# The low half of a weight unit on GpSimd: one instruction of 1024 columns, or two of 512

## The chip, the cores and the metric

The kernel runs on one core of a Trainium2 chip, as one launch. A core has a tensor engine (PE; its weight loads are listed apart as PEld), a vector engine (DVE), a scalar engine (ACT), GpSimd (POOL) and a sync engine (SP), which here only issues DMAs. The engines run their own instruction streams in order and wait for each other by semaphores. They share one on-chip memory of 128 partitions; matmul results go to a separate accumulation memory that POOL doesn't read here.

The metric is the time of one execution on the device in microseconds, the median over runs. Lower is better.

## The reference, cut to what matters

Attention that keeps only the 32 largest scores of each row, then a mixture of four experts, then a layer that takes the largest of three products. All of it is float32.

```python
scores = scale * np.matmul(q, k.transpose(0, 1, 3, 2))      # 2 batches, 8 heads, 576 x 576
kth = np.partition(scores, -32, axis=-1)[..., -32:-31]
attn = softmax(np.where(scores >= kth, scores, -1e9))
x = np.matmul(attn, v)                                      # -> 1152 tokens x 512
for e in range(4):                                          # w1[e] 512 x 1024, w2[e] 1024 x 512
    out += p[:, e:e + 1] * (np.maximum(x @ w1[e], 0.0) @ w2[e])
h = np.maximum(np.maximum(out @ m1, out @ m2), out @ m3)    # each 512 x 768
return h @ m_out                                            # 768 x 512
```

## The kernel before, in words

**High and low parts.** PE multiplies float32 operands in a format with fewer bits. To keep the accuracy, an operand is split in two: `hi`, a rounded copy that ACT writes, and `lo = raw - hi`, a subtraction. A product then takes three matmuls (`product`, L588 to L590): with the low part of one operand, with both high parts, and with the low part of the other. Tokens, hidden values and weights are all split so.

**Weight units.** The weights come as units of 128 x 1024 float32 (512 KB), 176 of them over the program. `w_units` lists them in the order in which the products use them. A unit goes through four steps:

1. SP loads it into one of three buffers (`raw`, L176). The load waits until the buffer's last readers are done, which are ACT's copy and the subtraction of the unit three places earlier.
2. ACT writes `whi` (L225, 1024 columns, one instruction).
3. POOL writes `wlo = raw - whi` (L229, 1024 columns, one instruction). From the phase with index `LATE` on (about two thirds of the way through the program), every second unit goes to DVE instead: POOL writes 136 units and DVE 40.
4. PE uses `whi` and `wlo` from one of five buffers each.

`weight` calls `w_split_to` for the unit wanted and four more (`W_AHEAD`), so that steps 1 to 3 stand in the program some units ahead of the products.

**The order of the work.** Nothing is reordered by a scheduler: each engine runs its instructions as the Python code emits them. `attention` runs through 36 pairs of heads and tiles in time slots. For each head of a pair, PE makes the scores, DVE finds the 32 largest by four MAX8 (L370) and three MATCH_REPLACE8 (L372) of 576 columns, ACT takes the exponential, and a mask sets what is too small to zero. For the first pairs the mask is POOL's (L393, L394); for the other 57 heads it is one DVE instruction (L390, `p = (s >= kth) * p`, which reads `s` and `p`, both in on-chip memory, and adds up the row). PE then transposes `p` (L408) and multiplies with the values.

Between the slots `products` emits the matmuls of the experts and of the last layer. How many go between two slots is decided by a clock kept in Python, which adds up what DVE and PE are thought to take (`dve`, `pe`, `clock`). It knows column counts only, not waits. From slot 306 on the weights of the last layer, which come as 64-bit floats, are turned into 32-bit ones in 48 pieces (`to_float32`), by three DVE instructions of each (L199, L202, L205) and an integer addition on POOL (L208), and stored to a buffer in DRAM from which they are loaded as units later.

POOL's other work stands in the same stream as `wlo`: low parts of the tokens (`xl`, L474), of the keys and queries (`kT` L261, `ql` L293), of some hidden values (L661, L795) and small memsets.

**What the change and the prediction touch.** The subtraction in `w_split_to` (L229), its readers on PE (L588 for the second kind of unit, L590 for the first), the load that waits for it (L176), and the DVE instructions with two inputs from on-chip memory that run beside it (L390, L199, L202, L205, L229 on DVE).

Of the kernel before, what the change touches and what calls it, by code (L numbers as in the profile page):

```python
# [10 lines left out]
F32 = mybir.dt.float32  # L11
# [4 lines left out]
ALU = mybir.AluOpType  # L16
# [34 lines left out]
def kernel(  # L51
# [14 lines left out]
    nc = tc.nc  # L66
# [103 lines left out]
    def w_load_to(n):  # L170
        while w_pos["load"] < min(n, len(order)):
            key, src = order[w_pos["load"]]
            if key[1] in "cd" and narrowed[0] < WIDE * (narrow_at[key[2:]] + 1):
                return
            raw = wp.tile([P, 1024], F32, tag="raw", bufs=3, name="raw")
            nc.sync.dma_start(out=raw, in_=src)  # L176
            w_raw[key] = raw
            w_pos["load"] += 1
# [37 lines left out]
    def w_split_to(n):  # L216
        while w_pos["split"] < min(n, len(order)):
            w_load_to(w_pos["split"] + 1)
            if w_pos["load"] == w_pos["split"]:
                return  # L220
            key, src = order[w_pos["split"]]
            raw = w_raw.pop(key)
            hi = wp.tile([P, 1024], F32R, tag="hi", name="whi")
            lo = wp.tile([P, 1024], F32R, tag="lo", name="wlo")
            nc.scalar.activation(out=hi, in_=raw, func=AF.Copy)  # L225

            late = w_pos["split"] - w_index[PHASES[LATE][1], "c" if PHASES[LATE][0] == 2 else "a", 0, 0]
            on = nc.vector if late >= 0 and late % 2 else nc.gpsimd
            on.tensor_tensor(out=lo, in0=raw, in1=hi.bitcast(F32), op=ALU.subtract)  # L229
            f = 512 if key[1] in "bd" else 256  # L230
            w_hl[key] = (hi.rearrange("p (a f) -> p a f", f=f), lo.rearrange("p (a f) -> p a f", f=f))
            w_pos["split"] += 1
            w_load_to(w_pos["split"] + 2)

    def weight(key, oldest=None):

        w_split_to(w_index[oldest or key] + W_AHEAD)
        return w_hl[key]
# [585 lines left out]
    for s, done in attention():  # L824
        if s == 20:
            load_gates()
        if s == W_FIRST - 12:
            w_load_to(3)
        if W_FIRST <= s < W_FIRST + 16 and not (s - W_FIRST) % 4:
            w_split_to((s - W_FIRST) // 4 + 1)  # L830
        if s == W_FROM - 6:
            for i in range(AHEAD_S):
                wide_load(i)
        if s >= W_FROM + W_STEP * conv and conv < WIDE * len(wide):
            converting.append(to_float32(conv))
            conv += 1
        for x in list(converting):
            if next(x, 0) == 0:
                converting.remove(x)
        split_waiting()  # L840
        assert not any((x.c, x.hp) in done for x in waiting)
        x_ready.update(done)
        clock["goal"] += (clock["dve"] - before) * SHARE[min(phase[0], len(SHARE) - 1)]
        before = clock["dve"]
        while clock["pe"] < clock["goal"]:
            if not advance():
                clock["pe"] = clock["goal"]
# [67 lines left out]
```

## Time and profile before

| what | value |
| --- | --- |
| median of 3 runs | 808.96 us (807.49 to 810.57) |
| the profiled execution | 808.2 us |
| its span, first to last instruction | 806.4 us |
| mean granted TensorE clock | 0.943 of full speed |
| PE busy | 746.3 us, 93% |
| DVE busy | 683.8 us, 85% |
| POOL busy | 527.2 us, 65%, of which `wlo` 336.5 us in 136 instructions |
| ACT busy | 492.7 us, 61% |
| DMA | 126.24 MB, mean 157 GB/s |

The span is the stretch that the trace covers; the profiled execution took 1.8 us more than it. A matmul's busy time runs past the start of the next one, since they are pipelined, so PE's share is higher than the share of the time that its matmuls need. The shares are means over stages with different limits: attention ends at about 490 us, and the products run on to the end.

### The profile page before, as it was taken

The numbers are of one execution on the slowest core, as the hardware profiler recorded it, in microseconds if no ns is written. First come the engines' busy times: TensorE is split into PE (matmuls) and PEld (weight loads), VectorE is DVE, ScalarE is ACT, GpSimd is POOL, SyncE is SP. The second block draws the span as 40 slices with busy tenths as digits, with TensorE's granted clock in tenths as the row PEclk, the third lists the DMA queues.
The fourth block names the chain that finished last, engine by engine and source line by source line (L and its number), as shares of the span: only waits on it lengthen the run. The fifth ranks groups of instructions, "written<-read, shape, count | busy, mean of one in ns | idle before, by whom it ended". The sixth has DMA issues, their size and how long they took to land.

```text
span 806.4 us, 13973 instructions
## 1 busy us (share of the span) xinstructions
PE 746.3 (93%) x4942; PEld 663.2 (82%) x4942; DVE 683.8 (85%) x1242; ACT 492.7 (61%) x1027; POOL 527.2 (65%) x316
## 2 busy tenths in 40 slices
PE   3776799999999989999999999989999898999998
PEld 2454699888898879888888987879988697989996
DVE  6999989999999999999999996999999683445441
ACT  5666768677776775766777665665565444545541
POOL 2787968779888876668777685566565473555330
PEclk8556599999999999999999999999999899999999
DMA  3430245636545445253534364877777455656531
GB/s 98 117 106 13 68 131 147 190 117 173 174 137 171 135 146 151 88 169 112 161 126 146 112 188 152 270 249 250 245 251 243 157 178 167 232 165 208 178 102 40
DMA packets 50214, 126.24 MB, mean 157 GB/s; under 512 B 7904, under 2 KB 18144, under 8 KB 50144
## 3 DMA queue, kind: packets, MB, share of 16 engines
q1 hardware_dynamic: 41936, 116.69, 46.8%
q10 hardware_dynamic: 8208, 8.65, 3.1%
q8 instruction: 39, 0.64, 0.3%
q14 instruction: 31, 0.25, 0.1%
HBM read 116.67 MB, written 8.65 MB: 155 GB/s over the span
## 4 chain that ended last, share of the span: by engine, by line
DVE 41%; PE 35%; DMA 8%; issue 6%; POOL 4%; ACT 4%; SPq 2%; ACTq 0%; DVEq 0%; POOLq 0%
DVE m L370 14%; DVE work L372 13%; PE ps L588 9%; PE ps L590 9%; PE ps L589 9%; DVE p L390 6%; DMA narrow<-narrow 3%; POOL wlo L229 2%; DMA raw<-in_w_dram 2%; DVE h L668 2%; ACT whi L225 2%; SPq L246 2%; DMA kraw<-in_k_dram 1%; PE pso L590 1%; PE pso L588 1%
## 5 line engine op out<-in xcount | busy, mean ns | idle before, releaser
L229 POOL TENSOR_TENSOR wlo<-raw,whi 128x1024 fp32r<-128x1024 f32 x136 | 336.5, 2487 | 162.6 <-ACT whi L225 155.8
L225 ACT ACTIVATE whi<-raw 128x1024 fp32r<-128x1024 f32 x176 | 182.9, 1058 | 73.7 <-DMA raw<-narrow 23.8
L588 PE MATMUL ps<-xl,whi 128*128 128x256 f32 (+1 forms) x512 | 155.3, 303 | 1.7 <-DVE h L668 0.8
L370 DVE MAX8 m<-work 128x8 f32<-128x576 f32 x216 | 154.6, 742 | 0.1
L589 PE MATMUL ps<-xh,whi 128*128 128x256 f32 (+1 forms) x512 | 152.6, 298 | 0.0
L590 PE MATMUL ps<-xh,wlo 128*128 128x256 f32 (+1 forms) x512 | 152.6, 298 | 0.0
L229 DVE TENSOR_TENSOR wlo<-raw,whi 128x1024 fp32r<-128x1024 f32 x40 | 61.6, 1541 | 66.4 <-ACT whi L225 64.9
L372 DVE MATCH_REPLACE8 work<-m,work 128x576 f32<-128x576 f32 x144 | 106.4, 740 | 0.0
L588 PEld LDWEIGHTS ps<-xl,whi 128*128 128x128 f32 x512 | 99.0, 193 | 3.7 <-DVE h L668 1.3
L589 PEld LDWEIGHTS ps<-xh,whi 128*128 128x128 f32 x512 | 98.8, 193 | 0.9
L590 PEld LDWEIGHTS ps<-xh,wlo 128*128 128x128 f32 x512 | 98.7, 193 | 0.0
L590 PE MATMUL ps<-x2h,wlo 128*128 128x256 f32 (+1 forms) x288 | 85.4, 296 | 0.8 <-DVE wlo L229 0.8
L588 PE MATMUL ps<-x2l,whi 128*128 128x256 f32 (+1 forms) x288 | 85.3, 296 | 0.0
L589 PE MATMUL ps<-x2h,whi 128*128 128x256 f32 (+1 forms) x288 | 85.2, 296 | 0.0
L390 DVE SCALAR_TENSOR_TENSOR p<-s,m,p 128x576 f32<-128x576 f32 x57 | 81.0, 1422 | 0.0
L588 PE MATMUL ps<-wlo,h 128*128 128x512 f32 x192 | 77.7, 405 | 0.0
L590 PE MATMUL ps<-whi,h 128*128 128x512 f32 x192 | 75.3, 392 | 0.0
L589 PE MATMUL ps<-whi,h 128*128 128x512 f32 x192 | 75.3, 392 | 0.0
L408 PE MATMUL psp<-ident,p 128*128 128x128 f32 x288 | 50.8, 306 | 26.3 <-POOL p L394 15.4
L208 POOL TENSOR_TENSOR narrow<-narrow,raw 128x256 int32<-128x256 int32 x48 | 41.2, 858 | 44.7 <-DVE narrow L205 14.6
L349 PE MATMUL pss<-kT,ql 128*128 128x288 f32 x160 | 55.1, 358 | 13.9 <-DVE ql L293 7.6
L408 PEld LDWEIGHTS psp<-ident,p 128*128 128x128 f32 x288 | 38.3, 156 | 32.9 <-POOL p L394 18.9
(104 smaller groups left out, 1706.0 us busy)
## 6 DMA issues: line engine op xcount, KB each, us to landing
raw<-in_w_dram SPq DMA_DIRECT2D x128, 512.0 KB, 3.9
raw<-narrow SPq DMA_DIRECT2D x48, 512.0 KB, 3.8
raw<-in_m_dram SPq DMA_DIRECT2D x36, 256.0 KB, 4.4
narrow<-narrow ACTq DMA_DIRECT2D x48, 128.0 KB, 3.7
kraw<-in_k_dram SPq DMA_DIRECT2D x14, 288.0 KB, 4.5
raw<-in_mo_dram SPq DMA_DIRECT2D x12, 256.0 KB, 4.2
vt<-in_v_dram SPq DMA_DIRECT2D x8, 288.0 KB, 4.2
out_dram<-ob ACTq DMA_DIRECT2D x9, 256.0 KB, 2.0
```

The source lines that it names most:

```text
L208: nc.gpsimd.tensor_tensor(out=out.bitcast(I32), in0=out.bitcast(I32), in1=last, op=ALU.add)
L225: nc.scalar.activation(out=hi, in_=raw, func=AF.Copy)
L229: on.tensor_tensor(out=lo, in0=raw, in1=hi.bitcast(F32), op=ALU.subtract)
L246: nc.sync.dma_start(out=out[half * D:(half + 1) * D], in_=src)
L349: nc.tensor.matmul(ps[:, 0:SH], lhsT=l, rhs=r, start=i == 0, stop=i == len(mm) - 1)
L370: nc.vector.max(m[:, 8 * r:8 * r + 8], src)
L372: nc.vector.match_replace(out=self.w[j], in_to_replace=m[:, 8 * r:8 * r + 8], in_values=src, imm_value=NEG)
L390: nc.vector.scalar_tensor_tensor(out=p, in0=s, scalar=kth, in1=p, op0=ALU.is_ge, op1=ALU.mult, accum_out=total)
L408: nc.tensor.transpose(ps[:, r * P:(r + 1) * P], self.p[:, part, part * TAIL + r * P:part * TAIL + (r + 1) * P], ident)
L588: nc.tensor.matmul(ps, lhsT=lh, rhs=rl, start=first, stop=False)
L589: nc.tensor.matmul(ps, lhsT=lh, rhs=rh, start=False, stop=False)
L590: nc.tensor.matmul(ps, lhsT=ll, rhs=rh, start=False, stop=last)
```

## The change

The subtraction on POOL is made by two instructions, the first for columns 0 to 511 and the second for columns 512 to 1023 of the same unit. Where the subtraction is DVE's, it stays one instruction. Buffers, DMAs and all other work are the same.

```diff
             late = w_pos["split"] - w_index[PHASES[LATE][1], "c" if PHASES[LATE][0] == 2 else "a", 0, 0]
             on = nc.vector if late >= 0 and late % 2 else nc.gpsimd
-            on.tensor_tensor(out=lo, in0=raw, in1=hi.bitcast(F32), op=ALU.subtract)
+
+            for x in (slice(0, 512), slice(512, 1024)) if on is nc.gpsimd else (slice(0, 1024),):
+                on.tensor_tensor(out=lo[:, x], in0=raw[:, x], in1=hi[:, x].bitcast(F32), op=ALU.subtract)
             f = 512 if key[1] in "bd" else 256
```

Two lines are added, so a line below it has a number higher by two after the change. No engine's order changes; the waits do at three places.

POOL's stream, early in the first product phase, before (`DMAHW`, `Activation`, `PE` name the semaphores of the DMA queues, ACT and PE):

```order
62 L229 TENSOR_TENSOR wlo<-raw,whi 128x1024 [waits DMAHW3_49,Activation_49]
63 L229 TENSOR_TENSOR wlo<-raw,whi 128x1024 [waits DMAHW4_49,PE_49,Activation_49]
64 L229 TENSOR_TENSOR wlo<-raw,whi 128x1024 [waits DMAHW5_49,PE_49,Activation_49]
65 L229 TENSOR_TENSOR wlo<-raw,whi 128x1024 [waits DMAHW6_49,PE_49,Activation_49]
66 L293 TENSOR_TENSOR ql<-qraw,qh 128x2x256 [waits DMAHW2_49,DMAHW1_49,Activation_49]
```

The same place after the change:

```order
66 L231 TENSOR_TENSOR wlo<-raw,whi 128x512 [waits DMAHW3_49,Activation_49]
67 L231 TENSOR_TENSOR wlo<-raw,whi 128x512
68 L231 TENSOR_TENSOR wlo<-raw,whi 128x512 [waits DMAHW4_49,PE_49,Activation_49]
69 L231 TENSOR_TENSOR wlo<-raw,whi 128x512
70 L231 TENSOR_TENSOR wlo<-raw,whi 128x512 [waits DMAHW5_49,PE_49,Activation_49]
71 L231 TENSOR_TENSOR wlo<-raw,whi 128x512
72 L231 TENSOR_TENSOR wlo<-raw,whi 128x512 [waits DMAHW6_49,PE_49,Activation_49]
73 L231 TENSOR_TENSOR wlo<-raw,whi 128x512
74 L295 TENSOR_TENSOR ql<-qraw,qh 128x2x256 [waits DMAHW2_49,DMAHW1_49,Activation_49]
```

The first of the two carries the waits of the old one; the second has none.

PE's stream at the third unit, whose first four products use columns in the order of the unit, before:

```order
203 L590 MATMUL ps_1071<-xh,wlo 128x256 [waits Pool_49]
204 L588 MATMUL ps_1071<-xl,whi 128x256
205 L589 MATMUL ps_1071<-xh,whi 128x256
206 L590 MATMUL ps_1071<-xh,wlo 128x256
207 L588 MATMUL ps_1071<-xl,whi 128x256
208 L589 MATMUL ps_1071<-xh,whi 128x256
209 L590 MATMUL ps_1071<-xh,wlo 128x256
```

After the change:

```order
203 L592 MATMUL ps_1075<-xh,wlo 128x256 [waits Pool_49]
204 L590 MATMUL ps_1075<-xl,whi 128x256
205 L591 MATMUL ps_1075<-xh,whi 128x256
206 L592 MATMUL ps_1075<-xh,wlo 128x256
207 L590 MATMUL ps_1075<-xl,whi 128x256
208 L591 MATMUL ps_1075<-xh,whi 128x256
209 L592 MATMUL ps_1075<-xh,wlo 128x256 [waits Pool_49]
```

The first matmul with `wlo` now waits for the first half alone, and the one that reads columns from 512 on waits for the second. On SP the loads of later units wait for ACT's semaphore too, which before was covered by the wait for POOL's.

## Rows read from the trace of the kernel before

**Rows 1.** Busy time by stretch: us, PE, PEld, DVE, ACT, POOL, PEclk, DMA share, GB/s

```profile
85.00:190.00 105.00, 97.74 (x707) 87.09 (x707) 101.38 (x206) 74.39 (x167) 83.26 (x48) 0.92 0.45 134
190.00:490.00 300.00, 290.47 (x2210) 256.90 (x2209) 292.16 (x592) 206.88 (x452) 227.20 (x120) 0.99 0.50 149
490.00:640.00 150.00, 144.18 (x715) 128.37 (x715) 138.86 (x196) 86.24 (x168) 89.14 (x67) 0.99 0.71 228
640.00:740.00 100.00, 97.47 (x721) 92.54 (x721) 51.31 (x54) 48.61 (x65) 50.01 (x27) 0.98 0.57 190
```

**Rows 2.** The chain that ended last, by line, 190 to 490 us

```profile
by line: DVE m L370 28.9%; DVE work L372 26.4%; DVE p L390 17.2%; issue 5.2%; DVE h L668 4.4%; DVE acc L697 2.7%; PE ps L588 1.7%; DMA raw<-in_w_dram 1.7%; ACT whi L225 1.7%; PE ps L590 1.7%; PE ps L589 1.7%; DVE xt L461 1.2%; ACT pt L411 0
```

**Rows 3.** DVE's L390 as a group, 190 to 490 us: busy us, mean ns, idle before

```profile
L390 DVE SCALAR_TENSOR_TENSOR p<-s,m,p 128x576 f32<-128x576 f32 x43 | 60.2, 1401 | 0.0
```

**Rows 4.** DVE's L390 in order of time: start us, duration us

```profile
92.69 2.65 DVE L390 SCALAR_TENSOR_TENSOR p<-s,m,p 128x576 f32<-128x576 f32 x1
...
201.23 0.81 DVE L390 SCALAR_TENSOR_TENSOR p<-s,m,p 128x576 f32<-128x576 f32 x1
...
215.29 2.79 DVE L390 SCALAR_TENSOR_TENSOR p<-s,m,p 128x576 f32<-128x576 f32 x1
...
223.04 2.32 DVE L390 SCALAR_TENSOR_TENSOR p<-s,m,p 128x576 f32<-128x576 f32 x1
...
483.27 2.26 DVE L390 SCALAR_TENSOR_TENSOR p<-s,m,p 128x576 f32<-128x576 f32 x1
```

**Rows 5.** POOL in order of time: start us, duration us, in brackets idle time before

```profile
92.39 2.35 POOL L229 TENSOR_TENSOR wlo<-raw,whi 128x1024 fp32r<-128x1024 f32 x1
94.69 1.79 POOL L293 TENSOR_TENSOR ql<-qraw,qh 128x512 fp32r<-128x512 f32 x1
...
202.62 4.76 POOL L229 TENSOR_TENSOR wlo<-raw,whi 128x1024 fp32r<-128x1024 f32 x2 [2.06 <-ACT whi L225]
...
215.07 2.40 POOL L229 TENSOR_TENSOR wlo<-raw,whi 128x1024 fp32r<-128x1024 f32 x1
217.43 0.97 POOL L474 TENSOR_TENSOR xl<-xt,xh 128x128 fp32r<-128x128 f32 x1
...
222.33 5.29 POOL L229 TENSOR_TENSOR wlo<-raw,whi 128x1024 fp32r<-128x1024 f32 x2
227.58 0.46 POOL L474 TENSOR_TENSOR xl<-xt,xh 128x128 fp32r<-128x128 f32 x1
```

**Rows 6.** Durations by line, ns: min/median/max, first and last start us

```profile
L229 POOL TENSOR_TENSOR wlo<-raw,whi x136: 2351/2410/3290, 86.2 to 780.0; 128x1024 fp32r<-128x1024 f32 x136
...
L202 DVE TENSOR_SCALAR narrow<-raw x48: 277/730/2495, 491.9 to 659.4; 128x256 uint32<-128x256 uint32 x48
L205 DVE SCALAR_TENSOR_TENSOR narrow<-raw,narrow x48: 409/425/2628, 492.2 to 660.6; 128x256 uint32<-128x256 uint32 x48
...
L661 POOL TENSOR_TENSOR h<-raw,h x12: 1272/1294/1952, 127.3 to 493.6; 128x512 fp32r<-128x512 f32 x12
```

**Rows 7.** One matmul group of PE, 190 to 490 us: busy us, mean ns

```profile
L588 PE MATMUL ps<-xl,whi 128*128 128x256 f32 x284 | 82.4, 290 | 1.7 <-DVE h L668 0.8 <-ACT raw L659 0.5 <-ACT r L438 0.2
```

**Rows 8.** One matmul of that shape in the chain that ended last

```profile
102.89 0.12 PE ps L588
```

**Rows 9.** POOL's `wlo` as a group, 190 to 490 us: busy, mean, idle before

```profile
L229 POOL TENSOR_TENSOR wlo<-raw,whi 128x1024 fp32r<-128x1024 f32 x72 | 178.2, 2495 | 57.5 <-ACT whi L225 56.3 <-DMA raw<-in_w_dram 0.9
```

**Rows 10.** The chain that ended last, by line, 85 to 190 us

```profile
by line: POOL wlo L229 12.9%; issue 12.7%; PE ps L588 10.6%; PE ps L589 10.6%; PE ps L590 10.5%; DMA raw<-in_w_dram 10.2%; SPq L246 5.8%; PE psp L408 3.8%; DVE m L370 3.7%; PE pss L349 3.5%; PE psv L451 2.9%; DVE work L372 2.8%; POOL kT L26
```

**Rows 11.** PE's waits for `wlo` of L229, whole run: us, times

```profile
  PEld ps L590: 1.2, 2
  PE ps L590: 0.8, 2
```

**Rows 12.** PE's longest waits, 490 us to the end: us, times, longest us

```profile
PE ps L588 <- DVE acc L697: 5.4, 2, 3.2
...
PE ps L590 <- DVE wlo L229: 0.8, 2, 0.4
```

**Rows 13.** PE's longest wait, 190 to 490 us: us, times, longest us

```profile
PE psp L408 <- DVE p L390: 3.5, 3, 2.5
```

## The prediction

> **What bounds the kernel now.** I read the busy time by stretch first [rows 1]. From 190 to 490 us, the longest stage, DVE is busy for 292.16 of 300 us and PE for 290.47; POOL has 73 us to spare. From 490 us on PE is the fullest engine (144.18 of 150 us, then 97.47 of 100). The chain that ended last says the same of the long stage: DVE's top-32 and mask lines L370, L372 and L390 alone are 72.5% of it, and L390 is 17.2% [rows 2]. The reader is to see there that `wlo` on POOL is not in the chain of this stage, so that making `wlo` slower or faster would not matter by itself.
>
> What matters is L390. Its 43 instructions take 1401 ns on the mean [rows 3], yet one of the same size takes 0.81 us when POOL is idle: it starts at 201.23 us [rows 4], and POOL's next instruction begins at 202.62 after 2.06 us of idle time [rows 5]. So 43 x (1.401 - 0.81) = 25.4 us of DVE's time in this stage is spent waiting inside L390. For what, the instructions side by side show. At 215.29 us L390 starts 0.22 us after a `wlo` on POOL and takes 2.79 us; that `wlo` is not lengthened (2.40 us) and ends at 217.47, and L390 ends 0.61 us later [rows 4, 5]. At 223.04 us it starts 0.71 us after a `wlo` and takes 2.32 us, again to some 0.6 us behind that `wlo`'s end [rows 4, 5]. DVE's instruction with two inputs from on-chip memory does not run beside POOL's: it waits until the POOL instruction under way is over. The turn then is DVE's, even with POOL's next instruction ready: the two `wlo` from 222.33 take 5.29 us together, 0.49 us more than 2 x 2.40, and the `xl` at 217.43 takes 0.97 us where the one at 227.58 takes 0.46 [rows 5]. POOL pays about 0.5 us for each such turn.
>
> **The change, part by part.** *What a half costs.* POOL's subtraction of 1024 columns has a median of 2.41 us, one of 512 columns (L661) of 1.29 us [rows 6]. Two halves are 2.58 us. Consecutive POOL instructions overlap a little: the one at 92.39 ends at 94.74 and the next has begun at 94.69, so 0.05 us comes off [rows 5]. A unit costs POOL 2 x 1.29 - 0.05 - 2.41 = 0.12 us, taken as 0.13, and 136 of them 17.7 us.
>
> *What DVE saves from 190 to 490 us.* A DVE instruction that comes during the first half now waits for 1.29 us at most instead of 2.41, so it is let through 1.12 us earlier. One that comes during the second half waits as before. In the old trace those of the first kind are the L390 that took over 0.81 + 1.12 = 1.93 us. I count ten of the 43, the first at 215.29 and the last at 483.27 [rows 4]: 10 x 1.12 = 11.2 us.
>
> *How much of it reaches the end.* PE is nearly as busy as DVE in this stage, and its matmuls are spread between the slots by a clock that doesn't know of DVE's waits, so they don't move. If DVE keeps its share, all 11.2 us go. If PE can't go above 99% busy, the stage takes 290.47 / 0.99 = 293.4 us and 6.6 us go. PE has in truth more room than that: a matmul of 256 columns is listed with 290 ns [rows 7], but in the chain one follows another after 0.12 us [rows 8], so its busy time covers small holes. I take the middle, **8.9 us**, and keep 3.5 and 11.2 as the ends: 3.5 us is what PE itself waits for L390 here [rows 13], the least that an earlier L390 gives back.
>
> *POOL in this stage.* 72 units x 0.13 = 9.4 us more, and 0.5 us for each turn that DVE now takes between two halves, ten of them. POOL sits idle for 57.5 us before its `wlo` here, nearly all of it waiting for ACT [rows 9]; that covers it. Without that cover, each unit would come 0.13 us later.
>
> *From 85 to 190 us.* Here POOL's `wlo` is the largest item of the chain, 12.9% of 105 us, some 5.6 units [rows 10]. These cost 5.6 x 0.13 = 0.7 us, and up to three turns of DVE in mid-unit 0.5 us each. Against that three L390 took over 1.93 us (the first, at 92.69 [rows 4], 2.65 us), worth 3.4 us of DVE's time, most of it not in the chain. I put this at 0, between 3.4 us gained and 2.2 us lost.
>
> *From 490 us on.* The conversion of the last weights has more such DVE instructions: L202 takes 277 ns at least and up to 2495, L205 409 and up to 2628 [rows 6]. DVE will be freer, but PE is the bound. What PE waits for DVE is 5.4 us in two waits for L697 and 0.8 us for DVE's own `wlo` [rows 12]. I take 1 us gained, between 0 and 6.2.
>
> *The new waits.* PE's first use of `wlo` now waits for half a unit, the later ones for the rest. PE lost 0.8 us to `wlo` of either engine in the whole run, and PEld 1.2 us [rows 11], since units are made some way ahead: at most that much to gain, nothing to lose. The extra wait on SP for ACT's copy has long been met when POOL's second half is done: 0.
>
> *The sum.* 8.9 + 0 + 1 = 9.9 us. The profiled execution took 808.2 us and would take 798.3. It is 0.76 us below the median of the runs, 808.96, to which I refer the forecast: **799.1 us**.
>
> **The rivals.** *(a) No gap between the halves.* All turns that the trace shows are given to DVE in front of a POOL instruction that has waits of its own. The second half has none. If it follows so closely that DVE isn't let in, DVE waits for both halves and each wait grows by 0.13 us: 35 of the 57 L390 begin inside a `wlo` (the first at 92.69, the last at 483.27 [rows 4]), 4.6 us, and 0.7 us on POOL's chain before 190 us: 808.96 + 5.3 = **814.3 us**, slower. What decides is whether DVE can start at all between two halves. Against it stands that the second of two `wlo` whose waits had been met let DVE in, and that such pairs overlap by the same 0.05 us [rows 5]. The Trainium skill (GPSIMD Engine Reference, section Instruction dispatch) speaks for it: each of GpSimd's cores begins the next instruction as soon as it has done its own share of the one before, and completion holds back only who waits for it. By that rule the sum would be that of this rival; the turn at 222.33 us [rows 5] is against it so far.
>
> *(b) PE takes over.* With PE at 290.47 of 300 us [rows 1], DVE's gain may turn into waiting for PE, at the next point where a score or a product is needed. Then only PE's own 3.5 us of waiting for L390 [rows 13] come off: **805.5 us**, no change within the bound below. For it: the two engines' near equal load. Against it: the holes inside PE's busy time [rows 7, 8].
>
> *(c) All of it counts.* PE's stream closes up, the stage gives its 11.2 us, the last stages the 5.4 us that PE waits for L697 [rows 12], and the stage before 190 us 1 us: 808.96 - 17.6 = **791.4 us**.
>
> **How the numbers follow.** Forecast 64%, (b) 16%, (a) 11%, (c) 9%. Half a per cent, 4.0 us, is about what a measurement of this kernel can tell from no change, so 804.9 and 813.0 are the limits. The forecast and (c) are faster: 73%. (b) is no change: 16%. (a) is slower: 11%. The range reaches from 790 us, just beyond (c), to 807 us, just beyond (b); it leaves out (a) and the tails of the others, and holds the ends of the costly terms: 3.5 us gained in the long stage alone gives 805.5, all bounds on the good side together (11.2 + 3.4 + 6.2) 788.2, which I leave out.
>
> **What would show it.** In the new profile POOL's halves should have a median near 1.29 us and a sum some 18 us above the 336.5 us of now. L390 should fall from 1.40 us on the mean in the long stage to about 1.14 (11.2 us less over 43), and its longest from 2.79 us and more to about 1.8; a longest still near 2.8 means rival (a). Attention should end some 9 us earlier; if L390 is shorter and attention ends as late as now, with more waiting of DVE for PE or ACT, it is (b). POOL's idle time before `wlo` should shrink but stay well above zero; if it is gone, or PE's waits for `wlo` go up by several us, I have misjudged POOL's cover and the forecast is wrong.

## The result, and the profile after

| what | before | after |
| --- | --- | --- |
| median of 4 runs | 808.23 us (806.68 to 810.57) | 796.33 us (795.39 to 797.97) |
| ratio of the times, 95% interval | | 0.9857 [0.9831, 0.9883] |
| the profiled execution, its span | 808.2, 806.4 us | 795.39, 793.6 us |
| POOL's `wlo` | 336.5 us in 136 | 374.9 us in 272 |

The change is faster by 1.4%, 11.9 us. The forecast was 799.1 us in a range from 790 to 807. A line below the edit has a number higher by two: DVE's mask is L392, the subtraction L231.

Busy time by stretch after the change (columns as in [rows 1]):

```profile
85.00:190.00 105.00, 96.72 (x721) 86.08 (x722) 101.41 (x208) 75.22 (x170) 88.45 (x73) 0.96 0.46 137
190.00:490.00 300.00, 294.89 (x2248) 262.06 (x2248) 291.70 (x602) 214.15 (x464) 245.19 (x198) 1.00 0.51 150
490.00:640.00 150.00, 144.96 (x755) 130.38 (x754) 135.72 (x197) 86.11 (x166) 96.56 (x85) 0.99 0.76 242
640.00:740.00 100.00, 97.47 (x704) 91.04 (x703) 43.88 (x49) 45.83 (x60) 54.52 (x40) 1.00 0.54 182
```

In the long stage PE gets through 2248 matmuls in 300 us instead of 2210, and DVE through 602 instructions instead of 592. POOL is 18 us busier there.

The mask and the subtraction as groups, 190 to 490 us (busy us, mean ns, idle time before):

```profile
L392 DVE SCALAR_TENSOR_TENSOR p<-s,m,p 128x576 f32<-128x576 f32 x43 | 53.5, 1243 | 0.0
...
L231 POOL TENSOR_TENSOR wlo<-raw,whi 128x512 fp32r<-128x512 f32 x146 | 198.5, 1390 | 43.7 <-ACT whi L225 43.0 <-POOL narrow L208 0.5
```

The 43 masks take 53.5 us where they took 60.2 [rows 3]. POOL's idle time before `wlo` went from 57.5 [rows 9] to 43.7 us, so its cover was drawn on and is not used up.

Durations by line over the whole run (min, median, max in ns):

```profile
L231 POOL TENSOR_TENSOR wlo<-raw,whi x272: 1266/1299/2312, 86.0 to 768.6; 128x512 fp32r<-128x512 f32 x136
L202 DVE TENSOR_SCALAR narrow<-raw x48: 275/726/1390, 480.6 to 645.9; 128x256 uint32<-128x256 uint32 x48
...
L392 DVE SCALAR_TENSOR_TENSOR p<-s,m,p x57: 797/1287/1936, 92.5 to 474.2; 128x576 f32<-128x576 f32 x57
```

The longest mask is 1.94 us, against 2.79 us and more [rows 4]; the longest L202 fell from 2.50 [rows 6] to 1.39 us. Nothing on DVE waits for a whole unit any more. L202 reads one tensor (`high`), though the section on the kernel before and the prediction take it for an instruction with two inputs. It waits all the same: before, 35 of its 48 instructions took over 0.4 us, where the least is 0.28, and each of these ends 0.15 or 0.16 us behind the end of a POOL instruction.

How the turn is taken, in order of time (start us, duration us), POOL first and then DVE's masks:

```profile
214.53 3.04 POOL L231 TENSOR_TENSOR wlo<-raw,whi 128x512 fp32r<-128x512 f32 x2
217.53 0.46 POOL L476 TENSOR_TENSOR xl<-xt,xh 128x128 fp32r<-128x128 f32 x1
...
214.54 1.89 DVE L392 SCALAR_TENSOR_TENSOR p<-s,m,p 128x576 f32<-128x576 f32 x1
...
221.38 1.26 DVE L392 SCALAR_TENSOR_TENSOR p<-s,m,p 128x576 f32<-128x576 f32 x1
```

This is nearly the place of the mask at 215.29 in [rows 4]. The mask comes as POOL starts a unit; the first half, at its median of 1.30 us, ends at 215.83, and the mask ends at 216.43, 0.60 us behind it. Before, a mask ended 0.61 us behind the whole unit. The two halves together take 3.04 us, 0.49 us more than 2 x 1.30 - 0.05: POOL's second half waited for the mask. The `xl` behind them takes its plain 0.46 us, where it took 0.97 [rows 5]. The turn has moved from the unit's end to its middle. This is no single case: of the masks from 190 to 490 us, the 27 before and the 28 after that took over 0.9 us all end 0.61 or 0.62 us behind the end of a POOL instruction.

The chain that ended last, by line, 190 to 480 us:

```profile
by line: DVE m L372 24.7%; DVE work L374 22.8%; DVE p L392 13.0%; PE ps L590 5.7%; PE ps L592 5.7%; PE ps L591 5.7%; DVE h L670 4.0%; issue 3.8%; PE psv L453 2.6%; DVE acc L699 2.1%; PE pss L351 1.8%; DMA raw<-in_w_dram 1.8%; PE psp L410 1.
```

DVE still leads, with the mask at 13.0% instead of 17.2% (the window before is 190 to 490 us, since attention ended later there), but PE's three products have gone from 5.1% [rows 2] to 17.1%: the two engines now share the stage's end.

Where the time came from: I take three marks, the starts of the 16th and of the 57th (last) mask and the end of the span. Before they are 201.23 and 483.27 [rows 4] and 806.4 us; after, the two masks are

```profile
200.25 0.81 DVE L392 SCALAR_TENSOR_TENSOR p<-s,m,p 128x576 f32<-128x576 f32 x1
...
474.20 1.31 DVE L392 SCALAR_TENSOR_TENSOR p<-s,m,p 128x576 f32<-128x576 f32 x1
```

So the way to the 16th mask gave 1.0 us, the stretch between the marks 282.0 - 273.9 = 8.1 us, and the rest 323.1 - 319.4 = 3.7 us: 12.8 us, the difference of the spans. The change run once more (below) has the marks at 203.6 and 476.5 of 795.8 us, which is -2.4, 9.1 and 3.8 us. The first part is thus within what differs from run to run; the second and third repeat.

### The profile page after: what moved, and what is told of

Read it like the earlier page. It is cut to its first block, busy times and chain, and to the rows that moved or that the text cites. A ratio compares the mean times of both kernels' runs of the same rounds, so it can differ in the third digit from the quotient of the medians.

```text
span 793.6 us, 14150 instructions
## 1 busy us (share of the span) xinstructions
PE 737.1 (93%) x4942; PEld 656.4 (83%) x4942; DVE 666.1 (84%) x1242; ACT 492.8 (62%) x1027; POOL 557.5 (70%) x452
## 4 chain that ended last, share of the span: by engine, by line
DVE 44%; PE 33%; DMA 8%; issue 6%; POOL 4%; ACT 4%; SPq 1%; ACTq 0%; DVEq 0%; POOLq 0%
DVE m L372 16%; DVE work L374 14%; PE ps L590 8%; PE ps L592 8%; PE ps L591 8%; DVE p L392 6%; POOL wlo L231 3%; DMA raw<-in_w_dram 2%; ACT whi L225 2%; DMA raw<-narrow 2%; DVE h L670 2%; PE pso L592 1%; PE pso L590 1%; DMA raw<-in_m_dram 1%; PE pso L591 1%
## 5 line engine op out<-in xcount | busy, mean ns | idle before, releaser
L231 POOL TENSOR_TENSOR wlo<-raw,whi 128x512 fp32r<-128x512 f32 x272 | 374.9, 1406 | 140.2 <-ACT whi L225 129.0
L231 DVE TENSOR_TENSOR wlo<-raw,whi 128x1024 fp32r<-128x1024 f32 x40 | 57.4, 1435 | 76.5 <-ACT whi L225 71.9
L392 DVE SCALAR_TENSOR_TENSOR p<-s,m,p 128x576 f32<-128x576 f32 x57 | 73.4, 1288 | 0.0
L351 PE MATMUL pss<-kT,ql 128*128 128x288 f32 x160 | 55.0, 358 | 13.5 <-DVE ql L295 7.5
L410 PEld LDWEIGHTS psp<-ident,p 128*128 128x128 f32 x288 | 37.4, 153 | 30.3 <-POOL p L396 18.8
```

The lines of the kernel that those rows point to most:

```text
L231: on.tensor_tensor(out=lo[:, x], in0=raw[:, x], in1=hi[:, x].bitcast(F32), op=ALU.subtract)
L351: nc.tensor.matmul(ps[:, 0:SH], lhsT=l, rhs=r, start=i == 0, stop=i == len(mm) - 1)
L392: nc.vector.scalar_tensor_tensor(out=p, in0=s, scalar=kth, in1=p, op0=ALU.is_ge, op1=ALU.mult, accum_out=total)
L410: nc.tensor.transpose(ps[:, r * P:(r + 1) * P], self.p[:, part, part * TAIL + r * P:part * TAIL + (r + 1) * P], ident)
```

## The experiments

My theory (T): a mask waits for the POOL instruction under way, halves let DVE in earlier, and DVE's time in attention is the gain. The rivals: the gain comes from what an extra instruction does beside that (an earlier release of half a unit to PE, waits of a finer grain); or from the conversion after attention; or DVE's gain is capped by PE. All edits are to the changed kernel, on its loop `for x in ...` unless shown otherwise; each ratio is to the kernel before, run on the same chip.

**Quarters.**

```diff
-            for x in (slice(0, 512), slice(512, 1024)) if on is nc.gpsimd else (slice(0, 1024),):
+            for x in [slice(i, i + 256) for i in range(0, 1024, 256)] if on is nc.gpsimd else (slice(0, 1024),):
```

> Four instructions of 256 columns per unit on GpSimd. Theory T (DVE gets its turn at the end of each GpSimd instruction, so shorter ones make it wait less): the mask on DVE (0.81 us undisturbed, mean 1.40 us before and 1.24 us with halves in the stretch from 190 to 490 us) falls to 1.0 to 1.1 us; GpSimd pays about 0.4 us more per unit than with one instruction (55 us in all), which fills its idle time but for the stretch before 190 us; time 790 to 797 us. Rival P (PE or the loads gain because a unit's first columns are released earlier; DVE's waits have nothing to do with it): a further gain of about half the first, 788 to 792 us, with the mask unchanged at 1.24 us. Rival C (fewer slow-clock stretches of TensorE by chance): 796 to 808 us, unrelated to the mask.

Measured: 800.37 us, 0.9902 [0.9872, 0.9932], a miss: both the time and the mean mask, 1194 ns, lie above what T expects. (The time lies where chance with the clock would put it, too, but the six runs' clocks, 0.951 to 0.972, are those of the change, 0.950 to 0.973.) The masks did get shorter than with halves, the kernel's time didn't:

```profile
L231 POOL TENSOR_TENSOR wlo<-raw,whi 128x256 fp32r<-128x256 f32 x289 | 220.0, 798 | 27.8 <-ACT whi L225 24.2 <-DMA raw<-in_w_dram 2.8 <-PE ps L590 0.2
L392 DVE SCALAR_TENSOR_TENSOR p<-s,m,p 128x576 f32<-128x576 f32 x43 | 51.4, 1194 | 0.0
```

These are the groups from 190 to 490 us. POOL has 27.8 us of idle time left where the halves have 43.7: a quarter has a median of 742 ns, so a unit costs 4 x 0.742 - 3 x 0.05 - 2.41 = 0.41 us more than in one piece. And something new happened, in order of time:

```profile
439.46 7.74 POOL L231 TENSOR_TENSOR wlo<-raw,whi 128x256 fp32r<-128x256 f32 x11
447.14 0.48 POOL L476 TENSOR_TENSOR xl<-xt,xh 128x128 fp32r<-128x128 f32 x1
447.56 2.81 POOL L231 TENSOR_TENSOR wlo<-raw,whi 128x256 fp32r<-128x256 f32 x4
457.39 0.74 POOL L231 TENSOR_TENSOR wlo<-raw,whi 128x256 fp32r<-128x256 f32 x1 [7.02 <-ACT whi L225]
446.22 4.77 DVE L392 SCALAR_TENSOR_TENSOR p<-s,m,p 128x576 f32<-128x576 f32 x1
```

The mask that comes at 446.22 is kept out past the ends of several POOL instructions and ends at 450.99, 0.62 us behind the last of them (447.56 + 2.81 = 450.37), after which POOL is idle. It got no turn in between. (This execution took 806.69 us, the longest of the six.) Rival (a) of the prediction, refuted for the halves, does occur here, for single masks.

**A cut at column 64**, `(slice(0, 64), slice(64, 1024))`: an extra instruction and the same waits, but nearly the old length for a mask to wait for. No read of PE lies in the first 64 columns (it takes `wlo` by 128 or 512 columns), so this cut releases nothing to PE early.

> Two instructions per unit as in the change, but of 64 and 960 columns: the added instruction, its cost and its waits without a cut in the middle. Theory T: DVE's mask stays at 1.35 to 1.40 us, because 960 columns hold DVE almost as long as 1024; GpSimd's pair costs about 0.13 us more than one instruction; time 806 to 811 us. Rival that two instructions or the finer waits help by themselves: 795 to 799 us as with the change.

Measured: 810.23 us, 1.0005 [0.9983, 1.0026]. The masks, 190 to 490 us:

```profile
L392 DVE SCALAR_TENSOR_TENSOR p<-s,m,p 128x576 f32<-128x576 f32 x43 | 62.5, 1453 | 0.0
```

They are no shorter than the 1401 ns of [rows 3] (and a little longer than expected), and no time is gained. The extra instruction is worth nothing by itself; the length of the piece is what counts. The early release is tried below, with the second half first.

**Halves in attention alone, halves after it alone**, by `and late < 0` and `and late >= 0` behind `on is nc.gpsimd` (the second kind leaves attention's units whole).

> Halves only for the 96 units before DVE takes a share of the units, that is as long as attention runs; one instruction for the 40 later ones. Theory T with the split of the gain that the traces show (attention's end 11 us earlier, the rest 1 to 2 us): 797 to 800 us, mask 1.2 to 1.27 us. If the gain came mainly from the later stages: 804 to 808 us.

> Halves only for the 40 units on GpSimd after attention; one instruction for the 96 earlier ones. Theory T: mask 1.40 us as before, 806 to 809 us, since PE is the fullest engine there and DVE's shorter waits are covered. If the late stages carry the gain: 797 to 802 us.

Measured: 798.37 us, 0.9861 [0.9836, 0.9886], and 806.4 us, 0.9975 [0.9951, 0.9998]. The masks of the first, then of the second:

```profile
L392 DVE SCALAR_TENSOR_TENSOR p<-s,m,p 128x576 f32<-128x576 f32 x43 | 53.3, 1239 | 0.0
```

```profile
L392 DVE SCALAR_TENSOR_TENSOR p<-s,m,p 128x576 f32<-128x576 f32 x43 | 60.2, 1400 | 0.0
```

The gain lies in attention. The halves after it, where DVE's conversion runs beside them, are worth about a quarter of a per cent, with an interval that nearly reaches nothing.

**POOL without reads.** How much would be gained if DVE never had to wait for `wlo`? POOL writes zeros into `wlo` instead of subtracting, in one piece of 1024 columns. Of the edit, which is to the kernel before, the loop around it and the old subtraction behind `else` are not shown.

```diff
+                if on is nc.gpsimd:
+                    on.memset(lo[:, x].bitcast(F32), 0.0)
+                else:
```

> GpSimd fills the low parts of its 136 units with zeros by one memset of 1024 columns, which reads nothing, instead of subtracting; the low parts of these weights are left out of the products. It shows how much more DVE's waiting is worth than halves give back. Theory T: a GpSimd instruction that only writes does not hold DVE up, so the mask takes 0.81 us but for the few behind other GpSimd instructions, mean below 0.9 us from 190 to 490 us (18 us less of DVE's time than with halves). If DVE stays the bound of that stretch, attention ends 25 us earlier than before and the time is 778 to 786 us; if PE takes over, as its 294.9 busy us of 300 with halves suggest, 786 to 794 us. If the mask stays at 1.2 us or more, what DVE waits for is not the reading, and T needs mending.

Measured: 777.54 us, 0.9619 [0.9587, 0.9651], below both ranges that were expected. The mask and POOL's memset in order of time, then the mask's group and the stretch 190 to 490 us:

```profile
233.57 1.85 POOL L232 MEMSET wlo<- 128x1024 f32 x2
...
234.17 0.81 DVE L395 SCALAR_TENSOR_TENSOR p<-s,m,p 128x576 f32<-128x576 f32 x1
```

```profile
L395 DVE SCALAR_TENSOR_TENSOR p<-s,m,p 128x576 f32<-128x576 f32 x42 | 36.2, 862 | 0.0
```

```profile
190.00:490.00 300.00, 299.54 (x2269) 267.52 (x2268) 280.26 (x609) 217.35 (x469) 117.20 (x126) 1.00 0.51 156
```

The mask runs beside a memset in its plain 0.81 us. The chain from 190 us to the end of attention here is PE's:

```profile
by line: PE ps L595 23.1%; PE ps L593 22.9%; PE ps L594 22.9%; PE pss L354 8.7%; PE psv L456 8.2%; PE psp L413 6.5%; PE psv L459 3.0%; PE psr L441 2.0%; PE psp L418 0.8%; POOL h L666 0.7%; ACT whi L225 0.3%; ACT s L362 0.3%; ACT h L665 0.2%
```

From the 16th to the 57th mask (191.7 and 462.7 us) it takes 271.0 us, 11.0 less than before, with PE at 299.54 of 300 us. That is what PE leaves to be gained in this stretch; the halves' 8.1 and 9.1 us are most of it. The rest of this kernel's gain lies ahead of the 16th mask, which comes 9.5 us earlier than before, and behind attention. It does two things at once there, less work for POOL and no waiting of DVE, so it doesn't say which of them gives it.

**DVE's own units in halves too**: the condition `if on is nc.gpsimd else ...` is dropped.

> As the change, and DVE's own 40 subtractions in two halves as well, so that GpSimd gets a turn in their middle. Theory T: GpSimd waits less behind DVE, but in the stages after attention, where PE is the fullest engine; DVE pays some 0.1 us more per unit, 4 us in all, off the path: 795 to 798 us, the same as the change within the error. If turns matter there too, 792 to 794 us.

Measured: 801.7 us, 0.9919 [0.9887, 0.995], a miss. (The interval just overlaps that of the change in its second measurement below, so the loss against the change is at the edge of the noise.) DVE's subtraction as a group from 490 us on, first of this kernel, then of the changed one:

```profile
L231 DVE TENSOR_TENSOR wlo<-raw,whi 128x512 fp32r<-128x512 f32 x78 | 67.5, 906 | 67.7 <-ACT whi L225 64.4 <-issue 3.3
```

```profile
L231 DVE TENSOR_TENSOR wlo<-raw,whi 128x1024 fp32r<-128x1024 f32 x39 | 55.6, 1426 | 74.1 <-ACT whi L225 69.5 <-POOL wlo L231 3.1 <-issue 1.5
```

Two halves on DVE are 1.81 us on the mean against 1.43 for the whole. By their medians, 0.692 us for a half and 1.226 for a whole, the second instruction itself costs 0.16 us; the other 0.22 us is time beyond the medians, which I take for waits, since each half can meet a POOL instruction. Attention ends as with the change (the 57th mask at 475.9 us), so the loss lies behind it, in an execution of 804.89 us, the longest of its six.

**Thirds**, pieces of 352, 336 and 336 columns.

> Three instructions of 352, 336 and 336 columns. Theory T with two opposite terms: DVE's mask falls between that of halves (1.24 us from 190 to 490 us) and that of quarters (1.10 us without one outlier), GpSimd pays another 0.13 to 0.2 us per unit; quarters measured 800 us and halves 796 us, so 795 to 799 us. Outside that, the two terms do not explain the quarters.

Measured: 795.97 us, 0.9848 [0.9817, 0.9879]: the masks' mean goes down to 1218 ns, the time is that of the halves. One mask misses its turns here as well; in order of time:

```profile
373.75 5.36 POOL L231 TENSOR_TENSOR wlo<-raw,whi 128x352 fp32r<-128x352 f32 x6
379.06 0.47 POOL L476 TENSOR_TENSOR xl<-xt,xh 128x128 fp32r<-128x128 f32 x1
379.48 2.67 POOL L231 TENSOR_TENSOR wlo<-raw,whi 128x352 fp32r<-128x352 f32 x3
377.32 5.45 DVE L392 SCALAR_TENSOR_TENSOR p<-s,m,p 128x576 f32<-128x576 f32 x1
```

It ends at 382.77, again 0.62 us behind the end of POOL's run at 382.15.

**The second half first**, `(slice(512, 1024), slice(0, 512))`, so that PE's first matmul with `wlo` waits for both halves as before.

> The same two halves, the second half of the columns first, so that PE's first use of a unit waits for both and its early release is gone. Theory T: nothing is lost, 795 to 798 us, mask 1.2 to 1.27 us from 190 to 490 us, because PE waited 0.8 us for these units in the whole run. Rival P, early release: 802 to 808 us.

Measured: 797.98 us, 0.9877 [0.9847, 0.9906], with a mean mask of 1197 ns. PE's waits for `wlo` are 1.2 us in 4 and PEld's 2.1 us in 4, against 0.8 and 1.2 us in 2 each: less than 1.5 us in all. The early release of the first half is not the source of the gain.

**POOL's other long subtractions in halves too**: `ql` (L295) head by head, the hidden values' low part (L663) in two, beside the change. The second edit is not shown.

```diff
-        sub(out=l, in0=t[:, heads, 0:n], in1=h.bitcast(F32), op=ALU.subtract)
+        for j in range(h.shape[1]):
+            sub(out=l[:, j], in0=t[:, heads, 0:n][:, j], in1=h[:, j].bitcast(F32), op=ALU.subtract)
```

> The change, and GpSimd's low parts of the queries and of its hidden values in two instructions each as well (768 and 512 columns become 2 x 384 and 2 x 256). Theory T: the waits of DVE's mask behind these, 2.7 us in the change's trace from 190 to 490 us, fall by about 1.3 us, and those of the conversion behind the hidden values (5.7 us) by half, the latter off the path; GpSimd pays 31 x 0.13 = 4 us. 794 to 797 us, so not to be told from the change; mask 1.20 to 1.25 us. A gain of 4 us or more would mean that turns behind long instructions matter more than their sum says.

Measured: 796.8 us, 0.9867 [0.984, 0.9895]; the masks of 190 to 490 us fall further, below what was expected:

```profile
L393 DVE SCALAR_TENSOR_TENSOR p<-s,m,p 128x576 f32<-128x576 f32 x43 | 50.2, 1167 | 0.0
```

That is 3.3 us less of DVE than with the change, and none of it shows in the time of the whole. Between the marks some of it does: from the 16th to the 57th mask this kernel takes 271.8 us, the two traces of the change 273.9 and 272.9, and the kernel without POOL's reads 271.0. Here PE leads the chain from 190 to 480 us, with 46.5% for its three products:

```profile
by line: PE ps L593 15.5%; PE ps L591 15.5%; PE ps L592 15.5%; DVE m L373 11.8%; DVE work L375 11.2%; DVE p L393 5.9%; PE psv L454 5.2%; PE pss L352 4.9%; PE psp L411 4.3%; PE psv L457 1.9%; DVE h L671 1.7%; issue 1.6%; PE psr L439 1.4%; DV
```

What lies behind the 57th mask is 323.2 us, longer than the change's 319.4, in an execution of 800.5 us, the longest of its six.

**The change, the quarters and the thirds once more**, beside the last one; the latter two as one execution each. Was the long mask of the quarters chance, and what is the scatter?

> The change unaltered, in the same job as the others, for comparison with the kernels of earlier jobs: ratio to before 0.983 to 0.988, 794 to 798 us; mask 1.20 to 1.28 us from 190 to 490 us, none of its 57 instructions above 2.0 us.

> The quarters again, for one look. In their first trace one mask at 446 us took 4.77 us: GpSimd's next six instructions ran in front of it. If a turn is missed by the program's order, the same mask (the 52nd of 57) is above 4 us again; if it hangs on timing by nanoseconds, another one or none is. The rest of the masks as before, median 0.9 to 1.1 us, time 798 to 807 us.

> The thirds again, for one look. In their first trace one mask at 377 us took 5.45 us. As for the quarters: the same mask again if the program's order makes it, another or none if it hangs on timing. Time 794 to 800 us.

Measured: the change 796.96 us, 0.9872 [0.985, 0.9893], with a mask mean of 1223 ns and a longest of 1.94 us; quarters 800.53 us; thirds 793.95 us, with no mask over 2.07 us. In the quarters the mask at 446 us is not late this time, but another one is:

```profile
470.71 0.49 POOL L476 TENSOR_TENSOR xl<-xt,xh 128x128 fp32r<-128x128 f32 x1
471.12 2.85 POOL L231 TENSOR_TENSOR wlo<-raw,whi 128x256 fp32r<-128x256 f32 x4
...
471.32 3.27 DVE L392 SCALAR_TENSOR_TENSOR p<-s,m,p 128x576 f32<-128x576 f32 x1
```

The order of the instructions is the same in both runs, so which mask is missed is a matter of timing. In the six traces of kernels with halves of 512 columns in attention no mask missed a turn like that. The intervals of quarters and halves overlap, but all seven runs of the quarters took 799.5 us or more, and nine of the ten of the change 798.0 or less. What makes the quarters slower isn't settled, but the marks say where: in their two traces the stretch from the 16th to the 57th mask is 274.7 and 274.5 us, about 1 us longer than with the change, though the missed turns of 4.0 and 2.5 us lie in it; what follows is 325.0 and 321.1 us against 319.4 and 319.3. (The 16th mask comes at 205.2 and 203.2 us, against 200.3 and 203.6.) The larger part of the loss thus lies outside the stretch, above all behind attention, where no mask is left to miss a turn. POOL's 0.41 us per unit is there, but no run has it without the rest.

None of these kernels beats the change by more than the intervals tell, but for the one that leaves POOL's low parts out. Thirds are its equal.

## Why the prediction was right, point by point

**The mechanism held.** A mask waits for the POOL instruction under way and gets its turn at that one's end, between two halves as well. Cutting off 64 columns gives nothing, halves give the gain, the halves in attention give nearly all of it, and the order of the halves doesn't matter. POOL's turn loss of 0.49 us at 214.53 is the 0.5 us that the prediction read from [rows 5].

**Rival (a) fell.** The longest mask is 1.94 us, and the time is below the one before. The rule in the Trainium skill (GPSIMD Engine Reference, Instruction dispatch) that spoke for it, that a GpSimd core goes on when its own share is done, would, as the prediction read it, have let the second half follow unbroken. At 214.53 us the trace disagrees, with DVE's turn in mid-unit. Masks like the quarters' of 4.77 us are what rival (a) describes, for a few short pieces; whether that rule is their reason no run shows.

**The saving on DVE was mis-sized.** The step was ten masks by 1.12 us, 11.2 us from 190 to 490 us, and a mean of 1.14 us. Measured are 60.2 - 53.5 = 6.7 us and 1.243 us. The ten long masks, taken one by one in their order, did what was forecast: 25.3 us became 14.7, and 13.5 in the second run of the change. What failed is that I left the other 33 as they were. They went from 34.9 to 38.7 us (39.0 in the second run), which took back 3.8 of the 10.6 us. One that was free before and waits now, first before and then after:

```profile
252.86 0.81 DVE L390 SCALAR_TENSOR_TENSOR p<-s,m,p 128x576 f32<-128x576 f32 x1
```

```profile
249.47 1.63 DVE L392 SCALAR_TENSOR_TENSOR p<-s,m,p 128x576 f32<-128x576 f32 x1
```

Before, POOL's `wlo` had ended at 252.34; after, the mask comes 0.29 us behind the start of a half. A mask that is let in earlier puts the following work at another point of POOL's stream, and may meet an instruction there. In all, 27 of the 43 waited by more than 0.1 us before, 0.95 us on the mean, and after it is 28, by 0.67 us. That is near half of a 1.30 us piece, but half of a whole unit would be 1.2 us where 0.95 was measured, so half a piece is no rule that these traces bear out.

The count of ten was short, too. By the prediction's own reading a mask ends some 0.61 us behind POOL's instruction, so those over 1.12 + 0.61 = 1.73 us came in the first half, not those over 1.93: twelve, with the ones at 391.02 (1.85 us) and 429.18 (1.80 us). With them the forecast of the saving would have been some 2 us further off.

**How much of it reaches the end was mis-sized the other way.** I let 8.9 of 11.2 us through, because PE was at 290.47 of 300 us. In truth the masks from the 16th to the 57th became 6.9 us shorter (59.4 to 52.5) and the stretch 8.1 us; in the second run of the change 7.9 and 9.1 us. All of the saving counts. The 1.2 us beyond it is within the scatter of this stretch: halves after attention alone leave the masks at 59.4 us there, and yet it takes 280.6 us, 1.4 less than before. PE's 99% was no limit: without POOL's reads PE is at 299.54 of 300 us. (With the change it is at 294.89, still below 99%.) The two errors nearly cancel, 8.9 forecast and 8.1 or 9.1 measured; that this term came out is luck in part.

**Rival (b)** did not decide at two halves; its point lies further away. At the halves PE's products are 17.1% of the chain; with all halves (50.2 us of masks) they are 46.5% and the time falls no further, and without POOL's reads PE is the whole chain. The price at which PE takes over is 11.0 us in this stretch, not the 3.5 us that I took from [rows 13].

**POOL's cost.** A half has a median of 1.299 us, forecast 1.29. The sum rose by 38.4 us instead of 17.7. The halves themselves are 136 x (2 x 1.299 - 0.05 - 2.41) = 18.8 us, as forecast. The rest I take for turns, without having traced each: what the instructions take beyond their median is 272 x (1.406 - 1.299) = 29.1 us after, 10.5 us before (a sum of 338.3 less 136 x 2.41). I had counted ten turns in mid-unit at 0.5 us, some 5 us. The cover that I named, POOL's idle time, carried it (57.5 to 43.7 us).

**The small terms.** From 85 to 190 us I put 0 between 3.4 gained and 2.2 lost; the 16th mask came 1.0 us earlier and, in the second run, 2.4 us later. After attention I put 1 us; the rest behind the 57th mask is 3.7 us shorter, of which 2.2 us lie between that mask and the first conversion, which is still attention's end, and 1.5 us later. The experiments say the same of the 2.2: from the start of that mask to the first conversion (L202) it is 8.62 us before and 6.39 with the change, 6.41 with halves in attention alone and 8.62 with halves after it. PE's waits for L699 there are down to 4.4 from 5.4 us [rows 12]:

```profile
PE ps L590 <- DVE acc L699: 4.4, 2, 2.6
```

PE's and PEld's waits for `wlo` are what they were in [rows 11], as forecast:

```profile
  PEld ps L592: 1.2, 2
  PE ps L592: 0.8, 2
```

**Not the clock.** The mean granted clock is 0.973 after and 0.943 before, but the four runs after, at 0.973, 0.972, 0.970 and 0.950, took 795.39, 796.30, 797.97 and 796.35 us: the one at 0.950 is no slower. Of the 45 runs of the kernel before beside the experiments, the 21 with a clock below 0.955 took 808.5 us on the mean, the other 24 808.4.

## What to carry to other kernels

Where DVE is the bound and some of its instructions are longer than their shortest, set them beside POOL's instructions: if they end a fixed bit behind POOL's, cut POOL's long ones, as long as POOL has idle time, and expect the waits to shrink rather than to vanish (here from 0.95 to 0.67 us on the mean, for pieces of half the columns): instructions that were free before meet a piece now. Don't go on cutting: each extra instruction costs POOL its fixed 0.13 us and more in turns, quarters were slower than halves, and the cut of DVE's own instruction gained nothing and may have cost time. Before that, ask how far the next engine is away, not by its busy share (PE went from 97% to nearly 100%) but by a run in which the wait is gone altogether.

## What the runs showed of the hardware that I had not expected

DVE doesn't always get its turn. With POOL pieces of 0.74 us (256 columns) a mask was kept out for 4.0 us in one run and 2.5 us in another, and with pieces of 336 and 352 columns once for 4.6 us, each time until POOL's run of instructions ended; with pieces of 1.30 us never in the six traces with halves in attention. Why the short pieces do this was not tried.

A POOL instruction that only writes doesn't hold the mask up: beside a memset it took 0.81 us, as with POOL idle [rows 4]. The Trainium skill says the same (SBUF — State Buffer, Who interferes with whom): an instruction of DVE with two inputs from on-chip memory contends with one of GpSimd that reads there, not with one that only writes.

This doesn't hold for every instruction of DVE. In the same run a memset did keep L202 waiting, which reads one tensor:

```profile
486.66 0.96 POOL L232 MEMSET wlo<- 128x1024 f32 x1
...
486.94 0.83 DVE L202 TENSOR_SCALAR narrow<-raw 128x256 uint32<-128x256 uint32 x1
```

It takes 0.83 us, where its least is 0.28, and ends at 487.77, 0.15 us behind the memset's end, as it does behind POOL's subtractions. This is the one clear meeting of the two in that trace.
